# Gated attention and top-1 experts on one core: the gate moved in front of the second expert layer

## The chip, the cores and the metric

The kernel runs on one core of one Trainium2 chip. The time is the device time of one launch, in microseconds; "before" is the median of three runs. PE is the matmul engine (TensorE), DVE the vector engine, ACT the scalar engine, POOL GpSimd, and SP the engine that here only issues DMAs.

## The reference

```python
# attention: B, S, D = 8, 2816, 256; z has 64 columns
scores = scale * np.matmul(z, z.transpose(0, 2, 1))
attn = np.maximum(scores, 0.0) ** 2
x = (u * np.matmul(attn, v)).reshape(B * S, D)
# experts: N = 22528 tokens, E = 8 experts, F = 512
y_dense = np.maximum(x @ w1_dense, 0.0) @ w2_dense
logits = x @ w_gate
expert_idx = np.argmax(logits, axis=1)
...                                   # softmax of the logits
gate_w = probs[np.arange(N), expert_idx]
for e in range(E):
    mask = expert_idx == e
    h = np.maximum(x[mask] @ w1[e], 0.0)
    y_moe[mask] = gate_w[mask, None] * (h @ w2[e])
return y_dense + y_moe
```

Every token goes through the dense two layers and through those of one expert, whose result is scaled by the token's gate, a positive number.

## The kernel before

**Attention stage.** For each of 8 batches the scores are made (L383), squared after a ReLU (L398 to L413) and multiplied with v (L552). The result times u goes into `pays` as bf16 rows (L579). Routing finds for each token its expert, its gate and its place. A row of 288 two-byte words, 256 of the token, then the gate in fp32 and the token's number, is written by POOL with an indirect DMA into the DRAM tensor `xs`, where each expert has a region of its own (L697).

**Expert stage.** The tokens are taken back in tiles of 256. The first NT1 = 70 tiles each lie in one expert's region in one piece; the 22 tiles behind them (NT2) are made of two pieces of 128, and the last few may be skipped by a branch. The work of PE, ACT, DVE and SP is issued in the order in which it is written down (`manual_schedule`); each engine works through its own part of that order, and waits where a needed result is not there.

`slot(s, end)` writes down one tile's turn:

1. `up(xT, w1d)`: the dense first layer of tile s. Eight matmuls into `h_ps`, a PSUM tile of two banks, of which there are three (L909), and one ACT pass with ReLU into a ring buffer (L912).
2. `half(s - 2, 1)`: the second half (128 tokens) of tile s - 2, see below.
3. `fetch` of the tile nine ahead. SP reads the row's address from a table, issues a transposing DMA from `xs` into the ring `x` of ten buffers (L872) and a DMA that brings the gates and token numbers, 8 bytes per token, into `me` (L874). Tiles 0 to 2 are fetched before the stage begins. In each of the slots 0 to 5 two tiles are fetched (3 and 4, 5 and 6, ..., 13 and 14), and from slot 6 on one:

```python
for _ in range(2):
    if fetched[0] < min(NT, s + 1 + AHEAD) and s < end:
```

4. `expert(s + 1)`: DVE copies the next tile's expert weights into a ring (L897).
5. `up(xT, we)`: the expert's first layer of tile s, as in 1.
6. `half(s - 1, 0)`: the first half of tile s - 1.

`half(s, j)` multiplies both first-layer results with their second layers (L917): four matmuls add up the dense part in one half of a PSUM tile `yy` (one bank; there are two such tiles), four the expert's part in the other half. ACT copies the dense part to SBUF (L932), DVE multiplies the expert's part with the gate, a number per token and here per partition, and adds the dense part (L933). POOL scatters the 128 rows to the output (L935). For j = 0 POOL then copies the rows once more into a buffer that nobody reads (`pause`, L922).

In the first layers' result a token is a column and a hidden unit a partition; in the second layers' result a token is a partition.

POOL's order is not fixed by hand. In the first slots the last routing work and in some later slots leftover scatters into `xs` (L695, L697) stand between the tiles' work.

Of the kernel before, what the change touches and what calls it, by code (L numbers as in the profile page):

```python
# [19 lines left out]
def kernel(  # L20
# [26 lines left out]
    T2 = 256  # L47
    Q1 = nB // G - 2

    NT1 = -(-(Q1 * G * P - E * (T2 - 1)) // T2)  # L50
# [9 lines left out]
    WD = 2 * F + 4 * D  # L60

    xs = nc.dram_tensor("xs", (XROWS, ROW // 2), F32, kind="Internal")[:]


    uf = u.rearrange("b (p n) d -> p b n d", p=P)
# [7 lines left out]
    zpool = pool("zp", 2)  # L73
# [8 lines left out]
    late = {}  # L82
# [750 lines left out]
    ring = {}  # L833

    def rings():

        def buf():
            return aA.tile([P, nK, 4 * P], BF, name="ring", tag="A")[:].rearrange("p k c -> p (k c)")
        def cut(r, o, n, size):
            return [r[:, o + i * size:o + (i + 1) * size] for i in range(n)]  # L840

        one, two, three = buf(), buf(), buf()
        ring["w"] = cut(one, 0, 4, WD) + cut(three, 0, 4, WD)
        ring["x"] = cut(one, 4 * WD, 5, 2 * T2) + cut(three, 4 * WD, 5, 2 * T2)
# [4 lines left out]
        ring["ys"] = [a.bitcast(F32) for a in ring["ys"]]  # L849
        ring["idle"] = [zpool.tile([P, nK, dq], BF, name="zr", bufs=1)[:]  # L850
                        .rearrange("p k d -> p (k d)").bitcast(F32)]

# [2 lines left out]
    def take(name):  # L855
        if not ring:
            rings()
        turn[name] = turn.get(name, -1) + 1
        return ring[name][turn[name] % len(ring[name])]

    def fetch(s):

        x = take("x")
        me = mx.tile([P, 2, 2], F32, name="me", bufs=16)
        if s < NT1:
            R = nc.values_load(Rt[0][0:1, s:s + 1], engines=[ET.SP], min_val=0,
                               max_val=XROWS - T2,
                               skip_runtime_bounds_check_because="made by the table")
            xT = x.rearrange("p (c h t) -> p h c t", c=2, h=2)
            rows = xs[bass.ds(R, T2), :]  # L870
            for ins in (
                    nc.sync.dma_start_transpose(out=x.rearrange("p (c t) -> p c t", c=2),  # L872
                                                in_=rows.bitcast(BF)[:, 0:D]),
                    nc.sync.dma_start(out=me[:], in_=rows[:, P:P + 2].rearrange("(j p) c -> p j c", p=P))):  # L874
# [12 lines left out]
        return xT, me  # L887
# [10 lines left out]
            wes.append(we)  # L898
        return wes

    def up(xT, ws):

        h_ps = late["s"].tile([P, 4, 2, P], F32, name="h_ps", tag="s")
        n = 2 // len(ws)
        for i, w1 in enumerate(ws):
            hs = slice(i * n, (i + 1) * n)
            for f in range(4):
                for c in range(2):
                    nc.tensor.matmul(out=h_ps[:, f, hs, :], lhsT=w1(c, f), rhs=xT[:, hs, c, :],  # L909
                                     start=(c == 0), stop=(c == 1))  # L910
        h = take("h")
        nc.scalar.activation(h, h_ps[:].rearrange("p f h t -> p f (h t)"), AF.Relu)  # L912
        return h

    def down(y, k, h, w2, j):
        for f in range(4):
            nc.tensor.matmul(out=y[:, k, :], lhsT=h[:, f, j * P:(j + 1) * P],  # L917
                             rhs=w2(f), start=(f == 0), stop=(f == 3))

    def pause(src):  # L920

# [2 lines left out]
    def half(s, j):  # L924

        hd, he, we, me, ids = pend[s]
        we = we[j % len(we)]
        yd, ys = take("yd"), take("ys")
        y = late["y"].tile([P, 2, D], F32, name="yy", tag="y")
        down(y, 0, hd, lambda f: w2d[:, f, :], j)  # L930
        down(y, 1, he, lambda f: we[:, 2 * F + f * D:2 * F + (f + 1) * D], j)
        nc.scalar.copy(yd, y[:, 0, :])  # L932
        nc.vector.scalar_tensor_tensor(out=ys, in0=y[:, 1, :], scalar=me[:, j, 0:1],  # L933
                                       in1=yd, op0=ALU.mult, op1=ALU.add)
        ins = nc.gpsimd.indirect_dma_start(  # L935
            out=out, out_offset=bass.IndirectOffsetOnAxis(ap=ids[j], axis=0),
            in_=ys, in_offset=None, bounds_check=N - 1, oob_is_err=False)
        nodep(ins, ["out"], "out")
        if j == 0 and s < NT1:
            pause(ys)  # L940
# [9 lines left out]

    MAYBE = 2
    AHEAD = 9
    got, wes = {}, {}
    pend = {}

    def slot(s, end):

        if s < end:
            xT, me = got.pop(s)
            we = wes.pop(s)  # L960
            hd = up(xT, [lambda c, f: w1d[:, c, f * P:(f + 1) * P]])
        if s - 2 in pend:
            half(s - 2, 1)
            del pend[s - 2]
        for _ in range(2):
            if fetched[0] < min(NT, s + 1 + AHEAD) and s < end:
                got[fetched[0]] = fetch(fetched[0])
                fetched[0] += 1
        if s + 1 < end:
            wes[s + 1] = expert(s + 1)  # L970
        if s == 1:
            half(0, 0)
        if s < end:
            he = up(xT, [lambda c, f, w=w: w[:, c * F + f * P:c * F + (f + 1) * P] for w in we])
            pend[s] = (hd, he, we, me, tokens(s, me))
        if s > 1 and s - 1 in pend:
            half(s - 1, 0)
# [180 lines left out]
```

## Time and profile before

| | |
|---|---|
| median of 3 runs | 885.77 us (883.65 to 889.91) |
| profiled execution | 887.47 us, its span 885.8 us |
| PE busy | 864.5 us, 98% of the span |
| DVE, ACT, POOL busy | 701.2, 738.6, 485.2 us |
| attention stage | from 0 to about 563 us |
| expert stage | from about 563 us to the end |

The span is what the profile covers; the run's time has 1.7 us more around it. A line of the profile names an engine, the line of the kernel, the operation, what it writes and reads, how often it ran, the busy time, the mean of one in ns, and the idle time just before with what ended it. In a timeline a row is start, duration, engine, line and operation; SPq is SP's queue of DMA issues. PEclk is the share of the full TensorE clock that was granted.

### The profile page before, as it was taken

What the parts mean: (1) busy time and instruction counts of PE and PEld (TensorE: products, weight loads), DVE (VectorE), ACT (ScalarE), POOL (GpSimd) and SP (SyncE); (2) the same over time, 40 slices, a digit from 0 to 9 for tenths busy, and PEclk for the clock granted to TensorE, in tenths of its full rate; (3) what the DMA queues carried; (4) which work ended last, traced back from release to release, by engine and by line L of the source; (5) the groups of instructions that cost most, each with busy time, mean ns of one, the idle gap of its engine ahead of it and who ended that gap; (6) DMA issues with size and microseconds to landing.
All of it is one profiled execution on the core that took longest, in us unless ns stands there. A gap on an engine that the chain in (4) does not pass through costs nothing.

```text
span 885.8 us, 30592 instructions
## 1 busy us (share of the span) xinstructions
PE 864.5 (98%) x12257; PEld 759.7 (86%) x12257; DVE 701.2 (79%) x1320; ACT 738.6 (83%) x913; POOL 485.2 (55%) x532
## 2 busy tenths in 40 slices
PE   8999999999998999999999999999999999999996
PEld 5788888898886888888888888888888888889996
DVE  7999999998996999999998997656665445546664
ACT  7999998998996998998998997477777777777774
POOL 8203343434533534434434544488888888887665
PEclk9999999999999999999999999999999999999998
DMA  6795997998898899899899896555565555544333
GB/s 148 148 174 117 146 185 145 172 174 170 153 165 168 154 181 190 127 197 198 131 196 172 151 159 112 103 133 128 129 132 122 117 120 121 123 113 110 97 100 82
DMA packets 257871, 127.64 MB, mean 144 GB/s; under 512 B 225470, under 2 KB 232894, under 8 KB 257728
## 3 DMA queue, kind: packets, MB, share of 16 engines
q1 hardware_dynamic: 230112, 70.24, 47.6%
q0 software_dynamic: 27616, 55.44, 29.2%
q8 instruction: 96, 1.57, 0.8%
q14 instruction: 47, 0.39, 0.2%
HBM read 61.54 MB, written 37.16 MB: 111 GB/s over the span
## 4 chain that ended last, share of the span: by engine, by line
PE 73%; DVE 7%; issue 6%; POOL 6%; DMA 4%; ACT 3%; SPq 0%; POOLq 0%; DVEq 0%; ACTq 0%
PE o L552 37%; PE h_ps L909 14%; PE yy L917 13%; PE s L383 8%; POOL out_dram L935 5%; DMA xT<-pays 3%; DVE r L400 2%; DVE A L413 2%; ACT A L411 1%; POOL A L413 1%; PE lg L607 1%; ACT r L398 1%; DVE pays L579 1%; DMA out_dram<-ring,ix 1%; DVE zn L113 1%
## 5 line engine op out<-in xcount | busy, mean ns | idle before, releaser
L552 PE MATMUL o<-vb,A 64*128 64x256 bf16 x7744 | 493.7, 270 | 2.6 <-POOL A L413 1.8
L552 PEld LDWEIGHTS <-A 64*128 64x128 bf16 x7744 | 408.1, 94 | 53.9 <-POOL A L413 3.0
L697 POOL DMA_INDIRECT xs<-pays,pi x176 | 196.9, 1119 | 271.1 <-DVE pi L695 207.1
L398 ACT ACTIVATE r<-s 128x1024 f32<-128x1024 f32 x274 | 270.0, 1011 | 26.1 <-PE s L383 22.1
L411 ACT ACTIVATE A<-r 128x1024 bf16<-128x1024 f32 (+1 forms) x257 | 261.3, 1042 | 5.3 <-DMA A<-A 2.7
L912 ACT ACTIVATE ring<-h_ps 128x1024 bf16<-128x1024 f32 x180 | 183.9, 1023 | 89.2 <-PE h_ps L909 87.3
L413 DVE TENSOR_TENSOR A<-r 128x1024 bf16<-128x1024 f32 x167 | 201.8, 1221 | 5.8 <-DMA A<-A 4.0
L400 DVE TENSOR_SCALAR r<-s 128x1024 f32<-128x1024 f32 (+1 forms) x158 | 190.5, 1214 | 4.3 <-POOL A L413 1.8
L933 DVE SCALAR_TENSOR_TENSOR ring<-yy,me,ring 128x256 f32<-128x256 f32 x180 | 86.8, 482 | 123.0 <-ACT ring L932 86.3
L935 POOL DMA_INDIRECT out_dram<-ring,me x140 | 146.4, 1046 | 39.8 <-issue 23.5
L383 PE MATMUL s<-zT 64*128 64x512 bf16 (+1 forms) x944 | 157.9, 359 | 1.6 <-ACT zT L192 0.6
L917 PEld LDWEIGHTS <-ring 128*128 128x128 bf16 x1440 | 140.0, 98 | 16.2 <-issue 0.3
L917 PE MATMUL yy<-w2d,ring 128*128 128x256 bf16 x720 | 108.0, 273 | 0.1
L917 PE MATMUL yy<-ring 128*128 128x256 bf16 x720 | 108.0, 273 | 0.0
L909 PE MATMUL h_ps<-ring,w1d 128*128 128x256 bf16 x720 | 93.3, 273 | 0.8 <-DVE pays L579 0.8
L909 PE MATMUL h_ps<-ring 128*128 128x256 bf16 (+1 forms) x880 | 93.7, 253 | 0.0
L897 DVE COPY ring<-wall 128x2048 bf16 x110 | 80.7, 748 | 8.6 <-DVE ring L933 4.2
L909 PEld LDWEIGHTS <-ring 128*128 128x128 bf16 x880 | 74.3, 98 | 6.8
L909 PEld LDWEIGHTS <-w1d 128*128 128x128 bf16 x720 | 70.1, 98 | 9.0 <-issue 1.0
L579 DVE TENSOR_TENSOR pays<-o,ut 128x512 bf16<-128x512 f32 x88 | 60.3, 685 | 17.6 <-PE o L552 17.1
L383 PEld LDWEIGHTS <-zT 64*128 64x128 bf16 x944 | 58.0, 94 | 16.0 <-issue 3.4
L932 ACT COPY ring<-yy 128x256 f32<-128x256 f32 x180 | 66.1, 367 | 1.8 <-PE yy L917 1.8
(120 smaller groups left out, 358.0 us busy)
## 6 DMA issues: line engine op xcount, KB each, us to landing
ut<-in_u_dram SPq DMA_DIRECT2D x88, 256.0 KB
vb<-in_v_dram POOLq DMA_DIRECT2D x16, 384.0 KB
vb<-in_v_dram POOLq DMA_DIRECT2D x16, 320.0 KB
wall<-in_moe_w_dram POOLq DMA_DIRECT2D x16, 256.0 KB
xs<-pays,pi POOLq DMA_INDIRECT x176
zr<-in_z_dram POOLq DMA_DIRECT2D x7, 352.0 KB
out_dram<-ring,me POOLq DMA_INDIRECT x140
A<-A SPq DMA_TRANSPOSE x128
```

What stands on the lines that cost most here:

```text
L383: nc.tensor.matmul(out=s[:, h, y * c:(y + 1) * c], lhsT=zT[r, k + h, :], rhs=zT[r, i0:i0 + w, :], start=True, stop=True)
L398: nc.scalar.activation(r[:, :, :c], s[:, :, :c], AF.Relu, scale=1.0 / S)
L400: nc.vector.tensor_scalar(out=r[:, :, :c], in0=s[:, :, :c], scalar1=1.0 / S, scalar2=0.0, op0=ALU.mult, op1=ALU.max)
L411: nc.scalar.activation(a, r, AF.Square)
L413: (nc.gpsimd if eng == "pool" else nc.vector).tensor_mul(a, r, r)
L552: nc.tensor.matmul(out=o[:, j, 0:D], lhsT=A[n][r, k, c:c + P], rhs=v_of[b][r, k, :], start=(p == 0 and x == 0), stop=(p == 1 and x == nK - 1))
L697: ins = nc.gpsimd.indirect_dma_start(out=xs, out_offset=bass.IndirectOffsetOnAxis(ap=pi[:], axis=0), in_=pays[:, g % (2 * G), 0:ROW].bitca ...
L909: nc.tensor.matmul(out=h_ps[:, f, hs, :], lhsT=w1(c, f), rhs=xT[:, hs, c, :], start=(c == 0), stop=(c == 1))
L912: nc.scalar.activation(h, h_ps[:].rearrange("p f h t -> p f (h t)"), AF.Relu)
L917: nc.tensor.matmul(out=y[:, k, :], lhsT=h[:, f, j * P:(j + 1) * P], rhs=w2(f), start=(f == 0), stop=(f == 3))
L933: nc.vector.scalar_tensor_tensor(out=ys, in0=y[:, 1, :], scalar=me[:, j, 0:1], in1=yd, op0=ALU.mult, op1=ALU.add)
L935: ins = nc.gpsimd.indirect_dma_start(out=out, out_offset=bass.IndirectOffsetOnAxis(ap=ids[j], axis=0), in_=ys, in_offset=None, bounds_chec ...
```

## The change

For the tiles 4 to 69 (`inside`) the gate is applied before the second expert layer. It is positive, so it may be multiplied into the ReLU's result. There a token is a column, so the gates of a tile must stand as a row on every partition. Three DMAs bring them there:

- in `fetch`, ahead of the transpose, SP loads the tile's 256 gates (4 bytes from each row of `xs`) into one partition of a buffer, `row`;
- `put`, three slots before the tile's turn, writes that row from ACT's queue to a DRAM tensor `gs`;
- `spread`, two slots before the tile's turn, reads it from there, again from ACT's queue, onto all 128 partitions, into one of ten buffers.

The expert's first-layer ReLU becomes a DVE instruction, max with 0 and times the gates, in place of the ACT pass. In `half` the dense and the expert's second layer add up in one group of eight matmuls; both halves of a tile share one PSUM tile `yy`, one half of a bank each. ACT copies the sum directly into the buffer that POOL scatters; DVE's pass at L933 is left out. Tiles 0 to 3 and those from 70 on are as before.

```diff
+    def put(s):
+        if inside(s):
+            nc.scalar.dma_start(out=gs[s:s + 1, :], in_=ring["row"][0][s:s + 1, :])
+
+    def spread(s):
+        if inside(s):
+            gates[s] = take("g")
+            nc.scalar.dma_start(out=gates[s], in_=gs[s:s + 1, :].to_broadcast([P, T2]))
...
+            if inside(s):
+                ins = nc.sync.dma_start(out=ring["row"][0][s:s + 1, :],
+                                        in_=rows[:, P:P + 1].rearrange("t o -> o t"),
+                                        allow_slow_non_contiguous=True)
...
+        if gb is None:
+            nc.scalar.activation(h, h_ps, AF.Relu)
+        else:
+            nc.vector.scalar_tensor_tensor(out=h, in0=h_ps, scalar=0.0,
+                                           in1=gb.unsqueeze(1).to_broadcast([P, 4, T2]),
+                                           op0=ALU.max, op1=ALU.mult)
...
+        if j == 0 or not inside(s):
+            yy[s] = late["y"].tile([P, 2, D], F32, name="yy", tag="y")
+        y = yy[s]
...
+        if inside(s):
+            down(y[:, j, :], hd, wd, j, stop=False)
+            down(y[:, j, :], he, we2, j, start=False)
+            nc.scalar.copy(ys, y[:, j, :])
...
     def slot(s, end):
...
+        put(s + 3)
+        spread(s + 2)
         if s + 1 < end:
             wes[s + 1] = expert(s + 1)
```

`put` and `spread` stand between steps 3 and 4 of the slot.

More of the change, by code (lines that the diff above doesn't have):

```diff
@@ L62 @@
     xs = nc.dram_tensor("xs", (XROWS, ROW // 2), F32, kind="Internal")[:]
+    gs = nc.dram_tensor("gs", (NT1, T2), F32, kind="Internal")[:]
     uf = u.rearrange("b (p n) d -> p b n d", p=P)
@@ L849, in rings @@
         ring["ys"] = [a.bitcast(F32) for a in ring["ys"]]
+        more = [zpool.tile([P, nK, P], BF, name="zT")[:].rearrange("p k c -> p (k c)") for _ in range(2)]
+        ring["g"] = [a.bitcast(F32) for m in more for a in cut(m, 0, 5, 2 * T2)]
+        ring["row"] = [zpool.tile([P, nK, D], BF, name="vb")[:].rearrange("p k d -> p (k d)")
+                       [:, 0:2 * T2].bitcast(F32)]
         ring["idle"] = [zpool.tile([P, nK, dq], BF, name="zr", bufs=1)[:]
@@ L927, in half @@
         we = we[j % len(we)]
[L928 to L934, printed above, removed]
+        ys = take("ys")
+        if j == 0 or not inside(s):
+            yy[s] = late["y"].tile([P, 2, D], F32, name="yy", tag="y")
+        y = yy[s]
+        wd = lambda f: w2d[:, f, :]
+        we2 = lambda f: we[:, 2 * F + f * D:2 * F + (f + 1) * D]
+        if inside(s):
+            down(y[:, j, :], hd, wd, j, stop=False)
+            down(y[:, j, :], he, we2, j, start=False)
+            nc.scalar.copy(ys, y[:, j, :])
+        else:
+            yd = take("yd")
+            down(y[:, 0, :], hd, wd, j)
+            down(y[:, 1, :], he, we2, j)
+            nc.scalar.copy(yd, y[:, 0, :])
+            nc.vector.scalar_tensor_tensor(out=ys, in0=y[:, 1, :], scalar=me[:, j, 0:1],
+                                           in1=yd, op0=ALU.mult, op1=ALU.add)
         ins = nc.gpsimd.indirect_dma_start(
```

19 lines of the change are left out of this document (12 added, 7 removed).

## The prediction

> **What bounds the kernel now.** I read the page first, then the busy time by stretch, then the waits, the timelines of PE, ACT and SP at the start of the expert stage and in its middle, and the wait rows of the fetch lines. In the stretches (start:end, length, then busy time and count of PE, PEld, DVE, ACT, POOL, and PEclk, DMA share, GB/s):
>
> ```profile
> 556.00:566.00 10.00, 9.12 (x143) 7.75 (x138) 5.46 (x23) 2.03 (x4) 2.92 (x3) 1.00 0.53 99
> 566.00:600.00 34.00, 34.00 (x323) 30.48 (x322) 20.73 (x60) 25.43 (x41) 26.01 (x32) 1.00 0.57 126
> 700.00:770.00 70.00, 70.00 (x644) 62.74 (x642) 34.59 (x67) 51.61 (x81) 59.55 (x73) 1.00 0.53 119
> 770.00:800.00 30.00, 30.00 (x277) 26.89 (x276) 14.94 (x26) 22.19 (x35) 25.59 (x30) 1.00 0.45 121
> ```
>
> From 566 us to 800 us PE is busy all the time at the full granted clock: 644 matmuls in 70 us are 109 ns each. The waits of DVE and ACT there are slack:
>
> ```profile
> DVE ring L933 <- ACT ring L932: 64.2, 82, 1.3
> ACT ring L912 <- PE h_ps L909: 57.7, 125, 0.5
> ```
>
> So a faster DVE or ACT is worth nothing in this stage, and every microsecond for which PE stands still is lost. One steady slot, on PE and on ACT:
>
> ```profile
> 702.26 1.04 PE L909 MATMUL h_ps<-ring 128*128 128x256 bf16 x8
> 703.13 0.60 PE L917 MATMUL yy<-w2d,ring 128*128 128x256 bf16 x4
> 703.57 0.60 PE L917 MATMUL yy<-ring 128*128 128x256 bf16 x4
> 704.00 1.04 PE L909 MATMUL h_ps<-ring,w1d 128*128 128x256 bf16 x8
> 704.88 0.60 PE L917 MATMUL yy<-w2d,ring 128*128 128x256 bf16 x4
> 702.50 0.37 ACT L932 COPY ring<-yy 128x256 f32<-128x256 f32 x1
> 704.25 0.37 ACT L932 COPY ring<-yy 128x256 f32<-128x256 f32 x1
> ```
>
> A slot is four such quarters of 0.87 us, 3.49 us. The copy of one half starts at 704.25, 0.08 us after both groups of its tile have ended (703.57 + 0.60), although it reads the first alone: a tile's PSUM bank passes from PE to its reader as a whole.
>
> **The matmuls.** 32 per tile before and after; one group of eight in place of two of four. At 109 ns each: 0.
>
> **DVE and ACT.** Rows for the prices:
>
> ```profile
> L933 DVE SCALAR_TENSOR_TENSOR ring<-yy,me,ring 128x256 f32<-128x256 f32 x126 | 60.8, 482 | 92.7 <-ACT ring L932 64.2 <-issue 20.4 <-POOL zr L922 6.6
> L912 ACT ACTIVATE ring<-h_ps 128x1024 bf16<-128x1024 f32 x127 | 129.9, 1023 | 58.6 <-PE h_ps L909 57.7 <-issue 0.9
> L400 DVE TENSOR_SCALAR r<-s 128x1024 f32<-128x1024 f32 (+1 forms) x158 | 190.5, 1214 | 4.3 <-POOL A L413 1.8
> L579 DVE TENSOR_TENSOR pays<-o,ut 128x512 bf16<-128x512 f32 x88 | 60.3, 685 | 17.6 <-PE o L552 17.1
> ```
>
> DVE loses two passes of 0.48 us per tile and gets one of 1024 elements out of PSUM with two inputs: between 1.21 (L400, one input) and 1.37 (twice L579); I take 1.25. DVE has 3.49 us for it and was busy 34.6 of 70. The result is needed by the second layer 3.5 us after its first layer ended; cover enough, 0. Without that cover the excess over 3.49 us would be lost per tile. ACT loses a pass of 1.02 us and issues two DMAs instead. Neither engine is relieved.
>
> **SP.** Each fetch gets one more DMA ahead of its transpose: 256 pieces of 4 bytes. The nearest row is the gate-and-token load L874, 256 pieces of 8 bytes. SP's queue at the stage's start (fetches of tiles 3 and 4, then the transpose of tile 14, the tenth after that of tile 4):
>
> ```profile
> 567.58 1.20 SPq L872 DMA_TRANSPOSE ring<-xs  x1
> 568.99 0.42 SPq L874 DMA_DIRECT2D me<-xs  x1
> 570.14 1.21 SPq L872 DMA_TRANSPOSE ring<-xs  x1
> 571.55 0.42 SPq L874 DMA_DIRECT2D me<-xs  x1
> ...
> 595.23 1.24 SPq L872 DMA_TRANSPOSE ring<-xs  x1
> ```
>
> A fetch takes 2.5 us (25.09 for ten). The added issue costs 0.42 plus the 0.20 between a transpose's end (571.35) and the next issue (571.55): 0.62. In the steady stage 3.1 us per fetch still fit into 3.49. At the start they do not: slots 0 to 5 ask for two fetches each, and SP falls behind. Tile 14 is asked for in slot 5, and its transpose starts at 595.23, when PE is long in slot 9:
>
> ```profile
> 581.74 1.04 PE L909 MATMUL h_ps<-ring,w1d 128*128 128x256 bf16 x8
> 584.36 0.60 PE L917 MATMUL yy<-w2d,ring 128*128 128x256 bf16 x4
> 585.23 1.04 PE L909 MATMUL h_ps<-ring,w1d 128*128 128x256 bf16 x8
> 586.10 0.60 PE L917 MATMUL yy<-w2d,ring 128*128 128x256 bf16 x4
> ```
>
> (slot 6 begins at 581.74, its half of tile 5 at 584.36, slot 7 at 585.23, the other half of tile 5 at 586.10). Today nobody but the loads themselves waits for SP.
>
> **The new wait.** The operands of SP's transfers in the trace name eight completion semaphores, taken in turn, and ahead of each issue stands a wait for the earlier transfer of the same semaphore (the rows below: two such wait instructions per L874 issue, one of them for this).
>
> ```profile
> L874 SPq EVENT_SEMAPHORE  x108: 17/22/55, 602.4 to 771.2; - x108
> L874 SPq DMA_DIRECT2D me<-xs x54: 377/389/1914, 602.5 to 771.3; - x54
> ```
>
> Today this costs nothing, as eight transfers are four fetches. I assume that ACT's transfers take from the same eight, in program order. Then in slot 6, which asks for only one fetch, the spread of tile 8 stands eight places behind the transpose of tile 14 (put 9, three of fetch 15, spread 7, put 8, load 14, transpose 14). ACT waits in order for SP's backlog. Behind it on ACT stands the copy of tile 5's first half, for which PE waits before it writes the other half into the same bank.
> [...]
>
> Working: eleven added issues (tiles 4 to 14) at 0.62 put the transpose of tile 14 at 595.23 + 6.8 = 602.0. SP waited 5.5 us in that stretch, and part of this takes up the delay:
>
> ```profile
> SPq L872 <- PE h_ps L909: 2.4, 3, 1.2
> SPq L872 <- PE yy L917: 1.8, 3, 0.9
> SPq L872 <- ACT ring L932: 1.3, 1, 1.3
> ```
>
> Bounds 596.5 and 602.0; I take 601.0, as PE's side, for which SP waits, moves later too. To its landing: the first load of the kernel was used 2.16 us after its issue began,
>
> ```profile
> 0.82 1.82 SPq L156 DMA_DIRECT2D z<-in_z_dram  x4
> 2.98 0.43 DVE L177 CAST zn<-z 128x512 bf16<-128x512 f32 x1 [0.27 <-DMA z<-in_z_dram]
> ```
>
> of which about 0.45 were the issue (1.82 for four). So 1.21 for the transpose plus 1.7: landed at 603.9. Spread issue 0.62, the copy 0.08 + 0.37: PE goes on at 605.0 instead of 586.10: 18.9 us. Earlier waits of this kind (put 4 for the load of tile 4, put 5 for that of tile 6) are swallowed by it, because SP's time does not hang on them. After slot 6 SP needs 3.1 us per fetch, PE 3.49, and ACT is not caught again.
>
> The clock: after a PE wait of this length the trace shows half the clock for 3.4 us.
>
> ```profile
> 273.52 0.20 PE L607 MATMUL lg<-wg,xT 128*128 128x8 bf16 x2 [4.19 <-DMA xT<-pays]
> 273.60:277.00 3.40, 3.40 (x34) 2.48 (x36) 3.10 (x9) 2.00 (x4) 0.17 (x1) 0.50 1.13 267
> ```
>
> That is 1.7 us of work. [...]
>
> **The per-slot wait of ACT.** PE now needs the copy of a half before it writes the other half, one quarter later. In the steady rows the copy ends at 704.62 and the next second layer starts at 704.88: 0.26, less 0.08 for the signal, 0.18 to spare. ACT's two issues follow the copy released at 702.50: 1.24 us, until 703.74, 0.51 before 704.25. Together 0.69 of tolerance per slot; a single issue of 1.29, as SP has at times, is 0.87 longer than 0.62 and uses it up:
>
> ```profile
> 697.87 1.29 SPq L874 DMA_DIRECT2D me<-xs  x1
> ```
>
> Most L874 issues take 0.39, so I count 0.
>
> ```profile
> 878.07 0.60 PE L917 MATMUL yy<-ring 128*128 128x256 bf16 x4
> 881.34 0.97 POOL L935 DMA_INDIRECT out_dram<-ring,ix  x1 [0.83 <-issue]
> ```
>
> **Sum.** 18.9 + 1.7 = 20.6. The profiled execution took 887.47 (span 885.8 and 1.7 around it), so it would take 908.1; against the median of the runs, 885.77, it is 906.4. PE works until 878.7 and the tail only moves later. Own range: the transpose at 596.5 and no clock loss, 900; at 602.0 with landings 2 us later, 909.
>
> **Rivals.**
> The first half of tile 1 begins on PE here:
>
> ```profile
> 570.13 0.60 PE L917 MATMUL yy<-w2d,ring 128*128 128x256 bf16 x4
> ```
>
> Only the data wait, **892** (+6): ACT's transfers have semaphores of their own. Then only put 4 in slot 1 is early: it needs the new load of tile 4, issued at about 570.1, landed 572.3. Then issue 0.62, copy 0.45 and the 1.02 us pass: 574.4 instead of 570.13; 4.3 and one half-clock window of 1.7. For it: I only infer the sharing. Against it: the eight cover every SP transfer.
>
> ACT late in every slot, **918**: if one of the two issues takes 1.29 and 0.20 around it (SP's queue transposes at the same time), ACT is 0.18 late in 66 slots, +12 on top of the forecast; it decides from 1.93 us for both issues. For it: 1.29 and 1.91 occur on SP. Against it: the median of 0.39.
>
> Not slower, **883**: POOL's last scatters are fed by ACT directly, without the 0.48 us DVE pass. It counts if POOL carries a backlog out of tile 69; the span ends 7.1 us after PE, of which the last scatter and its landing are 4.5, so at most 2.6 us come back, and only if neither wait above exists. For it: the end's chain runs through POOL. Against it: in the tail POOL waits for DVE, so it has no backlog.
>
> **How the numbers follow.** Forecast 0.58, data wait alone 0.20, ACT late per slot 0.14, not slower 0.08. One per cent, 8.9 us, is about what a measurement of this kernel can tell from no change. Slower by more: 0.58 + 0.14 = 0.72. Within: 0.20 and half of the last, 0.24. Faster by more needs what no row offers: 0.04. The range from 888 to 923 takes in the data wait and most of the per-slot case.
>
> **What would show it.** Right: PE idle for some 9 us or more between about 585 and 605, released by ACT's copy; ACT's two issue lines there waiting for SP's transfers, not for their own data; PE busy all the time from 610 to 800 at 109 ns per matmul; a slice of half clock after the gap; DVE's pass at 1.2 to 1.4 us. Wrong: one gap of 4 to 5 us near 570 and none after (the data wait); gaps of some 0.2 us in each slot (ACT); a fetch of over 3.49 us on SP, which would make SP the bound.

## The result, and the profile after

The changed kernel takes 922.34 us (median of six runs, 918.59 to 929.82), the kernel before beside it 887.09 (six runs, 879.69 to 894.82): a ratio of 1.0425, with a 95% interval from 1.0362 to 1.0488. Slower, as forecast, but by 35 us instead of 20.6. The ratios here and below are formed from the runs in the faster of two states that an execution can fall into, so that a ratio can differ a little from the quotient of the two medians beside it.

The busy time by stretch of the kernel after (start:end, length, busy time and count of PE, PEld, DVE, ACT, POOL, then PEclk, DMA share, GB/s):

```profile
566.00:600.00 34.00, 21.83 (x173) 17.38 (x171) 16.22 (x46) 11.00 (x19) 15.93 (x19) 0.90 0.52 103
600.00:630.00 30.00, 24.97 (x210) 21.22 (x210) 13.81 (x24) 11.67 (x21) 18.77 (x24) 0.94 0.71 127
630.00:700.00 70.00, 69.43 (x637) 62.08 (x635) 45.47 (x72) 32.92 (x60) 59.23 (x73) 1.00 0.78 157
700.00:770.00 70.00, 68.21 (x621) 60.56 (x620) 36.04 (x45) 32.06 (x59) 58.97 (x73) 1.00 0.81 155
800.00:830.00 30.00, 25.23 (x225) 21.84 (x224) 12.98 (x15) 11.37 (x20) 16.83 (x21) 1.00 0.67 124
```

PE, busy in all 34 us of 566:600 before, stands still for 12 of them now, for 5 of the next 30, and again for almost 5 after 800. In the middle it is nearly full. The timeline of PE shows waits (start, duration, ..., in brackets the idle time before and what ended it):

```profile
571.89 1.01 PE L948 MATMUL yy<-w2d,ring 128*128 128x256 bf16 x4 [5.64 <-DVE ring L974]
583.18 1.03 PE L934 MATMUL h_ps<-ring 128*128 128x256 bf16 x8 [1.63 <-ACT ring L939]
594.46 0.60 PE L948 MATMUL yy<-w2d,ring 128*128 128x256 bf16 x4 [2.81 <-ACT ring L968]
601.00 0.60 PE L948 MATMUL yy<-w2d,ring 128*128 128x256 bf16 x4 [1.22 <-ACT ring L968]
606.17 0.60 PE L948 MATMUL yy<-w2d,ring 128*128 128x256 bf16 x4 [1.52 <-ACT ring L968]
612.06 0.78 PE L948 MATMUL yy<-w2d,ring 128*128 128x256 bf16 x4 [2.23 <-ACT ring L968]
...
821.10 0.60 PE L948 MATMUL yy<-w2d,ring 128*128 128x256 bf16 x4 [1.39 <-ACT ring L968]
830.45 0.73 PE L948 MATMUL yy<-w2d,ring 128*128 128x256 bf16 x4 [2.09 <-ACT ring L968]
```

L968 is ACT's copy of a finished half, L948 the second layer of the next half in the same bank. The first row is of another kind, and is taken up behind the experiments: L974 is DVE's pass for the tiles that the change leaves as they were (0 to 3). What held ACT up at the third and fourth row stands in its own timeline, and the transfer it waited for in SP's:

```profile
593.59 0.35 ACTq L879 DMA_DIRECT2D zT<-gs  x1
594.04 0.37 ACT L968 COPY ring<-yy 128x256 f32<-128x256 f32 x1 [3.67 <-DMA vb<-xs]
...
600.13 0.35 ACTq L879 DMA_DIRECT2D zT<-gs  x1
600.58 0.37 ACT L968 COPY ring<-yy 128x256 f32<-128x256 f32 x1 [4.52 <-DMA vb<-xs]
```

```profile
590.71 0.55 SPq L892 DMA_DIRECT2D vb<-xs  x1
591.45 1.22 SPq L897 DMA_TRANSPOSE ring<-xs  x1
592.87 0.43 SPq L899 DMA_DIRECT2D me<-xs  x1
...
597.25 0.55 SPq L892 DMA_DIRECT2D vb<-xs  x1
```

ACT issues the spread of tile 7 at 593.59, 2.88 us after SP issued the added load of a much later tile, and the spread of tile 8 at 600.13, again 2.88 us after SP's next load but one. Neither spread reads these loads. The operands say why: the trace gives for each transfer the semaphore that it raises and the one that its issue waits for. ACT's spread raises and waits for the same one that SP's load just before it raises (116 at 590.71 and 593.59, 117 at 597.25 and 600.13), so ACT first waits for that load. I followed this through the stage, taking for each put and spread the last transfer before it on its semaphore:

```
kernel after: transfer (slot s), time, semaphore: last transfer on it before
spread of tile  7 (slot  5) 593.59 116: load of tile 11        s+6
spread of tile  8 (slot  6) 600.13 117: load of tile 13        s+7
put    of tile 11 (slot  8) 610.61 104: transpose of tile 16   s+8
spread of tile 11 (slot  9) 616.76 101: token load of tile 17  s+8
put    of tile 30 (slot 27) 678.91 103: transpose of tile 35   s+8
put    of tile 68 (slot 65) 819.88 105: transpose, tile 73     s+8
```

From slot 8 on, the put and the spread of slot s follow a transfer of the fetch of tile s+8 (the put of slot 60 alone follows a spread). So ACT may go on only once that transfer has landed, 2.1 us after its issue at the earliest (the spread of slot 8). Beside the slots I use two measures, both worked out from the starts of instructions. SP's **lead** for a tile is the time from the start of its transpose to the start of its slot on PE. The **shift** of a slot is its start from the start of slot 0, less the same in the kernel before; so the attention stage, which varied by some us from run to run, is left out.

| kernel | lead at tile 14 | 35 | 68 | 80 | 89 | shift at slot 12 | 63 | 70 | 89 |
|---|---|---|---|---|---|---|---|---|---|
| before | 14.5 | 32.0 | 32.1 | 20.4 | 8.2 | 0 | 0 | 0 | 0 |
| after | 29.6 | 31.1 | 35.2 | 26.6 | 14.4 | 23.4 | 27.5 | 35.2 | 35.2 |

The 35.2 us are 23.4 by slot 12, 4.1 in small stalls until slot 63, 7.7 from there to slot 70, and nothing after the last changed tile.

### The profile page after: what moved, and what is told of

It is laid out like the page before. It is cut to its first block, busy times and chain, and to the rows that moved or that the text cites. A ratio compares the mean times of both kernels' runs of the same rounds, so it can differ in the third digit from the quotient of the medians.

```text
span 918.7 us, 30791 instructions
## 1 busy us (share of the span) xinstructions
PE 871.8 (95%) x12257; PEld 761.4 (83%) x12257; DVE 710.4 (77%) x1254; ACT 678.5 (74%) x847; POOL 482.1 (52%) x532
## 4 chain that ended last, share of the span: by engine, by line
PE 64%; issue 8%; DMA 8%; POOL 7%; DVE 6%; ACT 4%; SPq 3%; POOLq 0%; ACTq 0%; DVEq 0%
PE o L553 35%; PE yy L948 9%; PE h_ps L934 9%; PE s L384 8%; POOL out_dram L976 6%; DMA xT<-pays 2%; DVE r L401 2%; ACT A L412 2%; DVE A L414 1%; ACT r L399 1%; SPq L897 1%; DMA me<-xs 1%; DMA A<-A 1%; DMA zT<-gs 1%; POOL A L414 1%
## 5 line engine op out<-in xcount | busy, mean ns | idle before, releaser
L948 PEld LDWEIGHTS <-ring 128*128 128x128 bf16 x1440 | 141.4, 99 | 44.9 <-issue 27.3
L941 DVE SCALAR_TENSOR_TENSOR ring<-h_ps,zT 128x1024 bf16<-128x1024 f32 x66 | 80.8, 1224 | 113.6 <-PE h_ps L934 108.5
L939 ACT ACTIVATE ring<-h_ps 128x1024 bf16<-128x1024 f32 x114 | 116.6, 1025 | 58.5 <-PE h_ps L934 51.4
L968 ACT COPY ring<-yy 128x256 f32<-128x256 f32 x132 | 48.9, 370 | 114.7 <-PE yy L948 61.1
L948 PE MATMUL yy<-w2d,ring 128*128 128x256 bf16 x720 | 109.7, 276 | 24.2 <-ACT ring L968 16.5
L948 PE MATMUL yy<-ring 128*128 128x256 bf16 x720 | 109.8, 276 | 0.0
L934 PE MATMUL h_ps<-ring 128*128 128x256 bf16 (+1 forms) x880 | 96.9, 258 | 1.6 <-ACT ring L939 1.6
L934 PEld LDWEIGHTS <-ring 128*128 128x128 bf16 x880 | 75.9, 100 | 10.2 <-issue 1.8
L922 DVE COPY ring<-wall 128x2048 bf16 x110 | 78.6, 729 | 6.9 <-DVE ring L974 4.2
```

The source lines that it names most:

```text
L939: nc.scalar.activation(h, h_ps, AF.Relu)
L941: nc.vector.scalar_tensor_tensor(out=h, in0=h_ps, scalar=0.0, in1=gb.unsqueeze(1).to_broadcast([P, 4, T2]), op0=ALU.max, op1=ALU.mult)
L948: nc.tensor.matmul(out=y, lhsT=h[:, f, j * P:(j + 1) * P], rhs=w2(f), start=(start and f == 0), stop=(stop and f == 3))
```

## The experiments

Theory **A**: ACT's put and spread wait, through the completion semaphores that they share with SP, for the fetch of tile s+8; the kernel pays where SP is not far enough ahead. Rivals: **B**, the changed computation (the DVE pass, the single PSUM group); **C**, SP's queue with the added load; **D**, the put waits for the data of its row; later **E**, ACT's transfers are late on busy DMA engines whatever they are paired with. Times below stand beside the kernel before on the same chip.

| kernel | us | before | ratio | shift at slot 12 | 63 | 70 | 89 |
|---|---|---|---|---|---|---|---|
| computation alone | 884.53 | 883.63 | 1.0005 (0.9968 to 1.0042) | 0.0 | 0.0 | 0.0 | 0.0 |
| load alone | 905.69 | 883.63 | 1.0241 (1.0192 to 1.0290) | 0.9 | 0.9 | 0.9 | 19.5 |
| constant row | 922.68 | 883.63 | 1.0429 (1.0376 to 1.0483) | 22.6 | 26.4 | 34.8 | 34.8 |
| tiles 16 to 59 | 903.04 | 883.63 | 1.0200 (1.0124 to 1.0276) | 0.0 | 18.4 | 18.4 | 18.4 |
| no load | 907.05 | 888.71 | 1.0235 (1.0168 to 1.0302) | 14.6 | 14.6 | 19.9 | 19.9 |
| tiles 40 to 69 | 895.57 | 888.71 | 1.0090 (1.0052 to 1.0128) | 0.2 | 1.5 | 7.5 | 7.5 |
| tiles 4 to 59 | 910.64 | 888.71 | 1.0286 (1.0234 to 1.0338) | 22.7 | 23.0 | 23.0 | 23.0 |
| load for tiles 4 to 35 | 886.70 | 888.71 | 0.9969 (0.9932 to 1.0007) | 0.3 | 0.3 | 0.3 | 0.3 |
| change, 7 buffers, AHEAD 6 | 916.65 | 886.34 | 1.0309 (1.0227 to 1.0390) | 14.1 | 21.0 | 23.6 | 28.5 |
| before, 7 buffers, AHEAD 6 | 896.72 | 886.34 | 1.0114 (1.0068 to 1.0160) | 0.0 | 0.0 | 0.0 | 10.0 |

**Computation alone.** No load, no put, no spread; DVE multiplies by a constant row.

```diff
     def put(s):
-        if inside(s): nc.scalar.dma_start(...)
+        pass
     def spread(s):
-            gates[s] = take("g"); nc.scalar.dma_start(...)
+            gates[s] = ring["g"][0]
...
-            if inside(s): ins = nc.sync.dma_start(out=ring["row"][0][s:s + 1, :], ...)
```

> The changed kernel without its three DMAs: the gates of tiles 4 to 69 are a constant row of ones, so the scaling by the gate is left out there; DVE's ReLU times gates, the group of eight matmuls and ACT's copy stay. Theory A (the loss is ACT waiting, through the shared completion semaphores, for SP's queue): 884 to 890, PE without a gap from 566 to the tail. Rival B (the computation itself costs: DVE's 1.22 us pass, or the copy that must come before the other half in the same bank): 900 to 922, gaps in every slot.

The two kernels cannot be told apart, and no slot moves. B falls. The stretch from 600 to 630 us of this kernel is full:

```profile
600.00:630.00 30.00, 30.00 (x277) 26.82 (x276) 21.14 (x34) 13.67 (x26) 24.95 (x32) 1.00 0.62 128
```

**Load alone.** As above, but SP's added load stays; put and spread are left out.

> As the compute-only kernel (gates are ones), with SP's load of the gate row put back, though nobody reads it; put and spread are left out. Theory A: 884 to 892, since SP falls further behind at the start but only the loads themselves wait for it. Rival C (SP's longer queue is itself the cost, tiles come too late): over 900, PE waiting for the transposes.

Here A missed: it had the load for nothing, and it costs 22 us. The start is not where they go (shift 0.9). SP's timeline in the middle of the stage:

```profile
690.31 1.25 SPq L896 DMA_TRANSPOSE ring<-xs  x1
...
693.70 1.22 SPq L896 DMA_TRANSPOSE ring<-xs  x1
...
697.04 1.23 SPq L896 DMA_TRANSPOSE ring<-xs  x1
...
700.49 1.23 SPq L896 DMA_TRANSPOSE ring<-xs  x1
```

A fetch takes 3.39 us (10.18 for three), PE's slot 3.49, so SP hardly gains: its lead is 5.8 us at tile 14 and 10.8 at tile 68, where before it is 32.1. From tile 70 on a fetch has two pieces and takes longer than a slot; before, the lead falls there from 32.1 to 8.2 us. Without it PE waits for the tiles themselves:

```profile
840.12 1.29 PE L933 MATMUL h_ps<-ring,w1d 128*128 128x256 bf16 x8 [2.15 <-DMA ring<-xs]
...
868.83 1.03 PE L933 MATMUL h_ps<-ring,w1d 128*128 128x256 bf16 x8 [2.36 <-DMA ring<-xs]
```

C is true as a cost of its own, but it puts the loss after slot 70, where the change has none.

**Constant row.** Every transfer of the change is issued, but put sends a row of ones, so no put waits for its load's data; the gates are left out.

```diff
-            nc.scalar.dma_start(out=gs[s:s + 1, :], in_=ring["row"][0][s:s + 1, :])
+            nc.scalar.dma_start(out=gs[s:s + 1, :], in_=ring["row"][1][s:s + 1, :])
```

> All three DMAs as in the change, but put writes a constant row of ones instead of the row that SP loads (the scaling by the gate is left out in tiles 4 to 69): ACT needs no data of SP's any more. Theory A (shared semaphores): as the changed kernel, 914 to 926, with ACT still released by SP's transfers. Rival D (ACT waits for the row's data): 886 to 896, no gaps at the start.

The same loss as the change within 0.4 to 1.1 us at each of the table's four slots, so D falls as the cause of the loss. (One wait of D's kind does stand in the change; see the part on the prediction.) The stalls are divided otherwise; this time one is over 9 us long, though later than the prediction had its single wait:

```profile
617.92 1.01 PE L950 MATMUL yy<-w2d,ring 128*128 128x256 bf16 x4 [10.49 <-ACT ring L970]
```

**Tiles 16 to 59.**

```diff
-        return FIRST <= s < NT1
+        return FIRST <= s < 60
-    FIRST = 4
+    FIRST = 16
```

> The change for tiles 16 to 59 instead of 4 to 69: no put or spread while SP works off its two fetches per slot, and none while it fetches the two-piece tiles. Theory A: 886 to 893, the start's 23 and the end's 8 us are gone and only some of the 4 us in the middle are left. Rival E (ACT is late by a little in all slots, or the computation costs): the loss goes with the number of tiles, 44 of 66, 908 to 912.

A miss: I had thought SP far enough ahead by then. It is 13.6 us ahead at tile 14, and over the next three tiles the lead is forced up to 23.9, 27.1 and 30.2; PE pays:

```profile
617.13 1.01 PE L948 MATMUL yy<-w2d,ring 128*128 128x256 bf16 x4 [8.20 <-DVE ring L974]
624.73 0.60 PE L948 MATMUL yy<-w2d,ring 128*128 128x256 bf16 x4 [2.23 <-DVE ring L974]
630.58 0.72 PE L948 MATMUL yy<-w2d,ring 128*128 128x256 bf16 x4 [2.19 <-DVE ring L974]
```

So the loss hangs on the lead at the place where puts and spreads begin, not on the start of the stage.

**Four kernels on another chip.** There the kernel before itself took 926.87 us (921.91 to 932.86), so only ratios can be read, and the expectations in us do not fit. All of the change but the load, with constant rows:

```diff
-            nc.scalar.dma_start(out=gs[s:s + 1, :], in_=ring["row"][0][s:s + 1, :])
+            nc.scalar.dma_start(out=gs[s:s + 1, :], in_=ring["row"][1][s:s + 1, :])
...
-            if inside(s): ins = nc.sync.dma_start(out=ring["row"][0][s:s + 1, :], ...)
```

> Put and spread from ACT for tiles 4 to 69 as in the change, but out of a constant row of ones, and SP's added load is left out (no scaling by the gate in these tiles): SP's queue is as before. Theory A, refined (through the shared semaphores ACT's spread in slot s waits for about the fetch of tile s + 8, so SP must be some 28 us ahead of PE as soon as put and spread begin; before, it is 5 to 15 us ahead there): 14 to 17 us of waiting at the start, half clock after it, and some 8 us where SP fetches two-piece tiles, 22 to 28 us slower, about 907 to 913. Rival C (all of the loss is SP's longer queue): as before, 883 to 889.

Measured 942.46, ratio 1.0161 (1.0125 to 1.0197). The change for tiles 40 to 69 (`FIRST = 40`) and for tiles 40 to 59 (`inside` ends at 60 as well):

> The change for tiles 40 to 69 only. Before, SP is its full 32 us ahead of PE from tile 35 on. Refined theory A: no wait when put and spread begin (slot 37), 1 to 2 us in the middle, and the 8 us at slots 63 to 69, 8 to 11 us slower, about 893 to 896. Rival E (a loss per tile): 30 of 66 tiles, 16 us, about 901.

> The change for tiles 40 to 59 only: neither the start nor the two-piece fetches are touched, and SP has its full lead before and after. Refined theory A: 0 to 2 us slower, 884 to 888. Rival E: 20 of 66 tiles, 11 us, about 896.

940.49, ratio 1.0148 (1.0104 to 1.0192), and 932.00, ratio 1.0055 (1.0023 to 1.0087). The added load issued twice, without put and spread:

```diff
-                ins = nc.sync.dma_start(out=ring["row"][0][s:s + 1, :], ...)
+                for r in (0, 1):
+                    ins = nc.sync.dma_start(out=ring["row"][r][s:s + 1, :], ...)
```

> As the load-only kernel (gates are ones, no put, no spread), with SP's load of the row issued twice per fetch into two rows. The load-only kernel lost 21 us, all from tile 75 on: SP never gets ahead and the two-piece tiles use up its small lead. Theory C as part of the whole (SP's queue is the bound there): a fetch takes 3.1 + 0.7 = 3.8 us, over PE's 3.49, so 66 more loads cost about 66 x 0.7 = 45 us more, about 945 to 955, and PE waits for transposes from the middle of the stage on. Rival (the load only disturbs the two-piece fetches' transfers): about 905 again.

959.26, ratio 1.0357 (1.0310 to 1.0403). Turned into ratios to the 885 us that the expectations stand on, A had 1.025 to 1.032, 1.009 to 1.012 and 1.000 to 1.002 for the first three, and none of the three lies there; the second lies between A and E's 1.018. For the fourth A and C together had 1.07 to 1.08, and 1.0357 is nearer to the rival's 1.02. The stage had waits of its own there, so these four decide nothing. The first two were run again on a chip like the first, with two new kernels.

**No load.** The same kernel as the first of these four.

> All of the change but SP's added load: the rows of gates that ACT puts and spreads are constant, so the gates are left out of the result. Relative to the kernel before on the same chip. Theory A (ACT's spread in slot s waits, through completion semaphores shared with SP, for about the fetch of tile s+8, and SP is too little ahead at the start): the start keeps most of its loss, since SP is only slightly earlier without the load: +14 to +20 us, ratio 1.016 to 1.023, all of it before slot 12. Theory C (SP's queue with the added load is the bound): 0 to +3 us, ratio 1.00 to 1.003.

A's numbers at the start: most of its loss is there without the load. SP fetches faster and so catches up at 14.6 instead of 23.4 us. From 600 us to slot 63 PE is full:

```profile
566.00:600.00 34.00, 25.50 (x188) 19.95 (x186) 14.97 (x36) 10.38 (x20) 16.86 (x19) 0.80 0.58 118
600.00:630.00 30.00, 30.00 (x277) 26.88 (x275) 20.35 (x34) 14.69 (x27) 25.17 (x30) 1.00 0.71 156
...
630.00:780.00 150.00, 150.00 (x1376) 134.35 (x1375) 86.82 (x122) 71.22 (x129) 127.12 (x157) 1.00 0.72 158
```

The semaphores of this kernel say more than was expected of it. From slot 8 to slot 60 its puts and spreads follow earlier puts and spreads on their semaphores, and no fetch; there it loses nothing (14.6 at slot 12 and at slot 63). From slot 61 on they follow the fetch of tile s+8 again, and 5.3 us are lost between slots 63 and 70, with no added load in SP's queue. So within one kernel the loss comes and goes with the pairing.

**Tiles 40 to 69.**

```diff
-    FIRST = 4
+    FIRST = 40
```

> The change for tiles 40 to 69 alone; the others keep the kernel before. By slot 36 SP is 32 us ahead of PE. Theory A: put and spread begin without a loss (0 to +2 us there), and the two-piece fetches of slots 63 to 69 cost what they cost in the change, +7 to +10: total +8 to +12, ratio 1.009 to 1.014. Theory C (the added load alone): 30 loads of 0.65 us take the lead from 32 to about 12 us at worst, and the two-piece tiles need 24: +5 to +12. A theory in which each tile costs the same share of the 35 us: 30/66, +16.

Puts begin with SP 31 to 32 us ahead, and slot 40 loses nothing. The cost comes in slots 64 to 69, 6.0 us, as in the change (7.7). C, too, had a total of this size; it is the place, ahead of the two-piece tiles' own slots, that speaks for A:

```profile
787.57 0.60 PE L948 MATMUL yy<-w2d,ring 128*128 128x256 bf16 x4 [1.04 <-ACT ring L968]
792.46 0.60 PE L948 MATMUL yy<-w2d,ring 128*128 128x256 bf16 x4 [1.24 <-ACT ring L968]
...
802.80 0.60 PE L948 MATMUL yy<-w2d,ring 128*128 128x256 bf16 x4 [2.59 <-ACT ring L968]
```

**Tiles 4 to 59.**

```diff
-        return FIRST <= s < NT1
+        return FIRST <= s < 60
```

> The change for tiles 4 to 59 alone; the two-piece tiles at the end keep the kernel before. Theory A: the start as in the change (+23), the middle as in the change (+2 to +4), and nothing in slots 63 to 69 by the coupling; the lead of 30 us or more that the coupling forced at the start is still there, so the two-piece tiles are covered as before: +25 to +29 us, ratio 1.028 to 1.033. If the loss at the end came from the load and not from the coupling: +30 to +35.

The start as in the change, and nothing after it: no slot from 51 on is paired with a fetch, and PE is full there.

```profile
800.00:850.00 50.00, 50.00 (x507) 45.34 (x506) 28.07 (x56) 36.55 (x59) 35.56 (x40) 1.00 0.41 105
```

**Load for tiles 4 to 35.** As the load alone, with

```diff
-            if inside(s):
+            if FIRST <= s < 36:
                 ins = nc.sync.dma_start(out=ring["row"][0][s:s + 1, :], ...)
```

> SP's added load alone, for tiles 4 to 35; no put, no spread, and DVE multiplies by a constant row, so the gates are left out of the result. Theory C' (the load alone costs because SP never builds the lead of 32 us that the two-piece tiles use up): after slot 36 SP gains 0.3 to 0.9 us per slot again and has 15 to 30 us by slot 70: 0 to +8 us, ratio 1.00 to 1.009. If instead each load costs its own time: 32/66 of 21, +10, with the loss before slot 36.

No loss. The lead, 6.4 us at tile 35, is 32.1 again at tile 65: an added load costs nothing if SP has the slots to win back its lead before the two-piece tiles.

**AHEAD = 6,** in the change and in the kernel before, meant to bring the paired fetch nearer.

```diff
-    AHEAD = 9
+    AHEAD = 6
```

> The whole change, but SP fetches 6 tiles ahead instead of 9 (AHEAD = 6). By theory A (eight semaphores in turn: 3 SP and 2 ACT transfers per slot) the spread in slot s now waits for about the fetch of tile s+5 instead of s+8, so SP has to be about 21 us ahead of PE instead of 31. The start then loses some 10 us less than the change: +11 to +15 by slot 12 instead of +23. The two-piece tiles use up 24 us of a lead of 21, so slots 63 to 91 lose +8 to +14. Against the kernel before on the same chip: +20 to +28, ratio 1.023 to 1.032. Theory E (ACT's transfers are late because they queue on the DMA engines behind other traffic, not behind a fetch at a fixed distance): the traffic is the same, so the start loses +20 to +24 as in the change.

> The kernel before with AHEAD = 6 and nothing of the change: the control for the run above. SP's lead stops at about 21 us, the start is unchanged, and the two-piece tiles use up 24: 0 to +5 us, ratio 1.00 to 1.006, all of it after slot 80. If it lost 10 us or more, the 32 us of lead would be needed by something else than the two-piece tiles.

919.20 (1.0399, 1.0332 to 1.0466) and 882.05 beside 884.53 (0.9979, 0.9935 to 1.0022): the change again and the kernel before again, with the leads of both (29.0 and 14.1 us at tile 14) and the same pairs on the semaphores. With ten buffers the pairing does not come from the place where the code asks for the fetch. How far SP runs ahead is set by the ten buffers of the fetched tiles: in the kernel before 32.1 us at most with AHEAD at 9 and at 6. The pair of runs tells nothing between A and E.

**7 buffers,** in the change and in the kernel before, with AHEAD at 9.

```diff
-        ring["x"] = cut(one, 4 * WD, 5, 2 * T2) + cut(three, 4 * WD, 5, 2 * T2)
+        ring["x"] = cut(one, 4 * WD, 5, 2 * T2) + cut(three, 4 * WD, 2, 2 * T2)
```

> The whole change, with 7 instead of 10 buffers for the fetched tiles, so that SP can be at most about 21 us ahead of PE instead of 32. In the trace of the change the put and the spread of slot s follow the fetch of tile s+8 on their semaphores. Theory A: with 7 buffers that fetch can be at most s+6, so the semaphores must pair them with an earlier fetch (about s+5), and the start loses some 10 us less: +11 to +15 by slot 12 instead of +23. The two-piece tiles then lose more, since they use up 24 us of lead: +10 to +16 in slots 63 to 91. Against the kernel before on the same chip +22 to +30. Theory E (ACT's transfers are late whatever the distance, for instance on busy DMA engines): +20 to +24 at the start as in the change.

> The kernel before with 7 buffers for the fetched tiles: the control for the run above. SP's lead stops at about 21 us; slots 0 to 69 keep their times, and the two-piece tiles, which use up 24 us, lose 0 to +6 us after slot 80. Ratio 1.00 to 1.007.

My error: with 7 buffers and AHEAD at 9 the fetch of tile s+9 is issued ahead of the slot that reads tile s+2 in the same buffer, so these two kernels compute on other tiles' tokens, and PE waits for fetches that it should not need. They took 956.24 (1.0785, 1.0690 to 1.0880) and 924.60 (1.0457, 1.0345 to 1.0570). With the change, the distance moved the other way: the put of tile 13 (slot 10) now follows the transpose of tile 22, s+12, and there stands a stall that neither the kernel without the change nor the change itself has; ACT first, then PE:

```profile
638.75 0.22 ACTq L873 DMA_DIRECT2D gs<-vb  x1
639.35 0.35 ACTq L879 DMA_DIRECT2D zT<-gs  x1
639.79 0.37 ACT L968 COPY ring<-yy 128x256 f32<-128x256 f32 x1 [13.30 <-DMA me<-xs]
```

```profile
640.22 1.01 PE L948 MATMUL yy<-w2d,ring 128*128 128x256 bf16 x4 [11.33 <-ACT ring L968]
```

**7 buffers and AHEAD = 6.** Both edits together; now each fetch comes after the last use of its buffer.

> The whole change with 7 buffers for the fetched tiles and AHEAD = 6, so that each fetch comes after the last use of its buffer (with 7 buffers and AHEAD = 9 it came before). SP can then be at most about 21 us ahead of PE. In the change the put and the spread of slot s follow the fetch of tile s+8 on their semaphores. Theory A: here they follow a fetch nearer by, about s+5, and the start loses +10 to +15 by slot 12 instead of +23; the two-piece tiles use up 24 us of a lead of 21 and lose +8 to +16. Total +20 to +30. Theory E (ACT's transfers late whatever the distance): +20 to +24 at the start.

> The kernel before with 7 buffers for the fetched tiles and AHEAD = 6: the control for the run above. The start is unchanged (0 to +1), SP's lead stops at about 21 us, and the two-piece tiles lose 0 to +6 us after slot 80: ratio 1.00 to 1.007.

The pairs on the semaphores, as above:

```
change, 7 buffers, AHEAD 6
put    of tile 15 (slot 12) 621.77 116: transpose of tile 17   s+5
put    of tile 21 (slot 18) 642.47 105: transpose of tile 23   s+5
```

The distance is five slots, the lead at tile 14 is 19.9 us instead of 29.6, and the start loses 14.1 us instead of 23.4, the 9.3 us that the lead is shorter (9.7). E had 20 to 24 there. Lead and loss go together: this shows A. What sets the distance itself is not shown: with 7 buffers it was s+12 at AHEAD = 9 and s+5 at AHEAD = 6. The middle of this kernel costs more than in the change (6.9 us from slot 12 to 63, not 4.1), and the two-piece tiles 7.5, just under what was expected. The control keeps its start and middle (shift 0.0 until slot 70) and loses 10.0 after slot 80, 4 more than expected: it has 21.6 us of lead at tile 68, the two-piece tiles use it up by tile 83 (4.7), and PE waits for the tiles as in the load alone:

```profile
854.42 1.05 PE L909 MATMUL h_ps<-ring,w1d 128*128 128x256 bf16 x8 [2.03 <-DMA ring<-xs]
...
873.91 1.05 PE L909 MATMUL h_ps<-ring,w1d 128*128 128x256 bf16 x8 [2.05 <-DMA ring<-xs]
```

## Why the prediction was right and wrong

**Matmuls, DVE, ACT at 0: right.** The computation alone has a ratio of 1.0005. DVE's new pass is close to the 1.25 us taken for it, and ACT's issues are shorter than the 0.62 taken for each:

```profile
L941 DVE SCALAR_TENSOR_TENSOR ring<-h_ps,zT 128x1024 bf16<-128x1024 f32 x66 | 80.8, 1224 | 113.6 <-PE h_ps L934 108.5 <-PE yy L948 5.1
L879 ACTq DMA_DIRECT2D zT<-gs x66: 349/350/422, 574.2 to 829.6; - x66
```

One reading behind this was weaker than it looked. That the copy at 704.25 starts behind both groups of its tile does not show that a bank passes as a whole, since ACT's pass ahead of it began at 703.33 and took 1.02 us. The kernel after shows it for one copy: at 573.79 ACT had been idle for 0.63 us when it copied a dense part, 0.04 us after the second group had ended (572.69 + 1.06) and 0.89 after the first (571.89 + 1.01).

**The shared semaphores: right, and now seen.** The prediction assumed them and found for slot 6 a transfer of tile 14, s+8. In the trace the pairs are s+6 and s+7 in slots 5 and 6 and s+8 from slot 8 on. ACT waits on semaphores for transfers of SP that its own do not depend on: in slot 6 the spread of tile 8 waits for 117, which SP's load for tile 13 raises, and is issued 2.88 us after that load (600.13 and 597.25).

**The start: the place right, the form wrong, the size 2.8 us short.** Forecast were one wait of 18.9 us at slot 6 and one half-clock window of 1.7, 20.6 in all; measured is 23.4. There is no single gap of 9 us or more. The longest wait, 5.64, is the data wait of the first rival: the put of tile 4 raises semaphore 117, whose last transfer SP had issued at 562.74, but its issue waits for 104, which the load of its own row raises. SP and ACT:

```profile
567.63 0.65 SPq L892 DMA_DIRECT2D vb<-xs  x1
```

```profile
570.43 0.48 ACTq L873 DMA_DIRECT2D gs<-vb  x1
570.95 0.37 ACT L973 COPY ring<-yy 128x256 f32<-128x256 f32 x1 [6.31 <-DMA vb<-xs]
```

The forecast had this wait at 4.3 us and swallowed by the later one, and swallowed it is: with constant rows this put does not wait, and the loss by slot 12 is 22.6 instead of 23.4. From slot 2 on the pairing holds and draws tighter (s+3, s+4, s+5, ...). So PE pays in nine waits up to slot 11, 17.2 us together (18.9 forecast in one), because it is the missing lead that is paid, however it is divided: PE loses time until SP is some 30 us ahead, and starts with 4. SP itself fell further behind than forecast: its transpose of tile 14 starts 40.5 us after slot 0 (601.12), against 32.3 before and 38.1 in the forecast, whose upper bound was 39.1. The clock is some 5 us of the rest: three windows at half speed instead of one, 1.7 us each. The last 1 us is no wait of its own. A matmul is listed with some 0.27 us, while in the full stage the next one starts after 0.11, so each bracket leaves out about 0.16 us of the wait (an estimate from these two figures; 1.4 for nine). The windows:

```profile
571.40:574.80 3.40, 2.91 (x14) 2.02 (x14) 3.11 (x16) 2.13 (x3) 1.93 (x4) 0.50 0.39 78
595.30:598.70 3.40, 3.40 (x18) 2.34 (x17) 1.36 (x2) 0.41 (x2) 2.16 (x3) 0.50 0.73 176
612.30:615.70 3.40, 3.40 (x19) 2.35 (x17) 0.26 (x1) 1.01 (x2) 2.36 (x3) 0.50 0.88 122
...
830.80:834.20 3.40, 3.40 (x19) 2.42 (x17) 0.42 (x1) 0.90 (x2) 2.25 (x3) 0.50 0.59 115
```

**"After slot 6 SP needs 3.1 us per fetch, PE 3.49, and ACT is not caught again": the step that failed.** It compared rates and forgot that the pairing stays for every slot and that the fetch s+8 changes its kind. From slot 62 on the partner is a tile of two pieces, and SP's timeline there shows what such a fetch takes:

```profile
822.37 1.19 SPq L910 DMA_TRANSPOSE ring<-xs  x1
823.83 0.36 SPq L911 DMA_DIRECT2D me<-xs  x1
824.38 1.17 SPq L910 DMA_TRANSPOSE ring<-xs  x1
825.77 0.48 SPq L911 DMA_DIRECT2D me<-xs  x1
827.57 1.21 SPq L910 DMA_TRANSPOSE ring<-xs  x1
...
832.13 1.20 SPq L910 DMA_TRANSPOSE ring<-xs  x1
```

Two tiles in 9.76 us (822.37 to 832.13) are 4.9 each, 1.4 over a slot. PE is held to SP's pace there, +7.7 with the fourth half-clock window; the runs with tiles 40 to 69 (6.0 from slot 63 on), without the load (5.3) and with tiles 4 to 59 (0) show that it is the pairing in just these slots. The 4.1 us of small stalls in the middle come with the same pairing when a transfer lands late: three of the four follow the spreads at 655.94, 724.42 and 771.12, which ACT issued 5.2 to 5.8 us after the token load that they are paired with, most others 3.2 to 4.5 after. Without the load, where the middle has no such pairs, it loses 0.0. But with tiles 4 to 59, with the same pairs up to slot 49, it loses only 0.3 (the change 3.0 by there); the pairing alone does not set the size, and what makes a transfer late was not tested. So 20.6 + 2.8 + 4.1 + 7.7 = 35.2.

**"In the steady stage 3.1 us per fetch still fit into 3.49": true, and not enough.** The fetch came to 3.39 us there. It fits, but SP does not fill its lead of 32 us, on which the two-piece tiles live. Alone this costs 22 us; in the change it costs nothing at the end, because the stalls at the start have already brought SP to 30 us (14.4 us left at tile 89, before 8.2). The two costs do not add up.

**The rivals.** The data wait alone (892) and the per-slot delay of ACT (918) fell: constant rows lose the same, and PE is all but full from 630 to 770 us. The 918 lay near the result for another reason, and it is luck that the result lies within 888 to 923: the upper part of that range stood for a delay of ACT in every slot, which no run shows. "A fetch of over 3.49 us on SP" was named as what would prove the forecast wrong; that came true for the two-piece tiles alone.

## What to carry to other kernels

A transfer given to a second queue can be tied to the first by shared completion semaphores, as the puts and spreads here from slot 8 on to the fetch of tile s+8: look up in the operands which semaphore each transfer raises and what came last on it, and compare the distance with how far the first queue really is ahead at that place. A queue that needs less time per slot than the bounding engine is still not free to load, if a later stretch lives on the lead that it builds (3.39 us per fetch in a slot of 3.49 cost 22 us with the load alone); ask how much lead is used up, not only whether a step fits into a slot. The tie cost the missing lead once (23.4 us by slot 12), and then again where the tied step became longer than the loop around it (4.9 us against 3.49: 7.7 us).

## What was not expected of the hardware

A wait of PE of 2.09 us (ahead of 830.45) was followed by 3.4 us at half the granted clock, where the trace of before showed it after 4.19. A longer one, the 2.59 ahead of 802.80 with tiles 40 to 69, was not: PEclk is 1.00 from 800 to 812 us. The clock records in the trace of after put its half-speed stretches ahead of the kernel's tail at 571.37, 595.26, 612.33 and 830.78, each 3.41 us long; they start 23.89, 17.07 and 218.45 us apart, which is 7, 5 and 64 times 3.413. In the 3.41 us ahead of each PE was busy for 0.00, 0.80, 1.18 and 1.32 us, so it had stood still throughout ahead of the first alone; 1.83, 1.91 and 1.91 us in the 3.41 from 581.61, 588.44 and 810.30 were followed by full speed. The busy time alone does not settle it: in the 3.41 us up to the end of the wait of 2.59 PE was busy for only 0.8, as its row before has eight matmuls from 799.18 for 1.04 us. What else decides was not shown. Half speed also lasted longer: eight matmuls took 1.86 us at 581.56 with constant rows and still 1.87 at 585.02; without the load 1.87 at 573.06 and 1.83 at 576.53 (1.04 at full speed), so for some 5 us at least in both.

With two more transfers per slot on ACT and one on SP, the DMA share rose from 0.53 to 0.81 (700 to 770 us), and these landed later: the output scatter took 3.82 us from issue to landing instead of 2.71, the transpose 3.73 instead of 3.04, and the token load 3.54 instead of 2.06 (medians over 620 to 780 us, from the last rise of each transfer's semaphore that the trace has).

On one chip the kernel before took 926.87 us where the others gave 883 to 889. The attention stage was the same there in the four kernels profiled (slot 0 at 562.5 to 564.2 us); in their expert stage PE waited for DVE and ACT (with tiles 40 to 59, 16.7 of the 140 us from 620 to 760), also in slots that the change does not touch. The cause was not found.
